# Attention's projection, value and output products as rolling pairs of row halves beside the scores

## The chip, the cores and the metric

The kernel runs on one core of a Trainium2 chip. The metric is the device time of one execution in microseconds (us), lower is better. Engines are named as in the profile: PE is TensorE's matmul, PEld its weight load, DVE is VectorE, ACT ScalarE, POOL GpSimd and SP SyncE, which issues DMAs.

## What is computed

Four layers in turn on x of 2048 rows and 512 columns, each added to its own input after a layer norm: a Fourier layer, an attention, the same Fourier layer, the same attention (`x = x + A(norm(x)); x = x + B(norm(x))`, twice). The Fourier layer is a product with two 512x512 matrices and then two 2048x2048 ones. The attention has 32 heads of 16 columns and four segments of 512 rows:

```python
q, k, v = x @ wq, x @ wk, x @ wv          # split into 32 heads, 4 segments
for s in range(4):
    p = softmax(qs @ ks.T * scale + mask)  # causal within the segment
    a_dot = p @ vs
    a_mem = (phi(qs) @ M) / (phi(qs) @ z + 1e-6)
    o = g * a_mem + (1 - g) * a_dot        # g = sigmoid(beta), per head
    M, z = M + phi(ks).T @ vs, z + sum(phi(ks))
return o @ wo
```

`phi(t)` is t + 1 above zero and exp(t) below.

## The kernel before

The program is laid out by hand on a clock of slots. `place(order, generator, times)` enters a generator at one or more times; at the end all entries run by time, and by `order` within a time, and each runs its generator up to the next `yield`. The matmuls and transposes are kept in the order in which they are so issued. The other engines' instructions are put in order by the compiler's scheduler, in which maxima and some copies have a raised priority. All PSUM tiles come from one pool of eight banks (`bank`).

The Fourier layers (`place_spectral`) are not touched. `place_attention` lays out one attention, from slot t0: 32 units of ten slots (SU = 10), a unit being four heads of one segment, so a segment (SS) is 80 slots. b is a segment's first slot. For each unit at slot t:

- `stack` (t-22) loads the heads' queries and keys with their low parts from DRAM, 48 rows for two heads at partition 0 and two at 64.
- `natural_max` computes scores with queries along partitions ("nat"), in five groups of two banks, and DVE takes each row's maximum with the mask (line 835). Two heads' matmuls run in the lower and upper half of the array's rows (`SIDES`).
- `max_rows` (t-5) turns the maxima into rows 48 and 49 of the query stack: a transpose `mT`, a copy `mt`, two DMAs.
- `softmax_values` computes the scores again, keys along partitions ("sT", 50 rows), in five groups at t, t+2, ..., t+8. ACT applies relu to the diagonal blocks and the exponential (lines 903, 904); POOL masks. At t+12 the 16 value products (`pv`, 32 output columns each, recorded as two matmuls apiece) follow, and a copy `ot`.
- `output` (t+14) transposes `ot` ("on") and divides.

For each segment there are `prep` (loads, normalises, transposes the rows into `xT`), `values` (four tiles `pvv`), `proj` (for four groups of heads g a tile each of q and k, `pqk`, followed by two copies, the feature map `phi` and DMAs to DRAM scratch), `mem_read` and `mem_update` (products with and into the state M, "pm", transposes "pkT", copy `pkn`, products "pM"), `transpose_out` ("oT") and `outproj` ("po", four tiles, plus the row added from `xr`). Numbers are held as a high and a low part, so each 128-row block takes three matmuls (`matmul3`), and a tile of 128x512 takes twelve. `matmul3` of projections, values and outputs stands three or six at a time in the slots between the scores, which are in every even slot.

The last segment of the second attention has its own tail (`outproj_split`, `transpose_last`), which is not changed.

Of the kernel before, what the change touches and what calls it, by code (L numbers as in the profile page):

```python
# [18 lines left out]
P = 128  # L19
# [39 lines left out]
def spectral_infini_kernel(  # L59
# [20 lines left out]
    def in_order(engine, name):  # L80
        op = getattr(engine, name)

        def call(*args, **kwargs):
            return tc.keep_in_program_order(op(*args, **kwargs))  # L84

        return call

    T = SimpleNamespace(matmul=in_order(T, "matmul"), transpose=in_order(T, "transpose"))
# [17 lines left out]
    def matmul3(ps, lhsT, rhs, first, last, **kw):  # L106
        T.matmul(ps, lhsT(0), rhs(0), start=first, stop=False, **kw)
        T.matmul(ps, lhsT(0), rhs(1), start=False, stop=False, **kw)
        T.matmul(ps, lhsT(1), rhs(0), start=False, stop=last, **kw)

# [570 lines left out]
    def place_attention(x_in, x_out, t0, w_at, out_at):  # L681
# [3 lines left out]
        def prep(s, n):  # L685
            xt = [load_rows(x_in[s * LT + i]) for i in n]
            yield
            mine = slice(s * LT + n[0], s * LT + n[-1] + 1)
            mv, rr = row_mv[:, mine], row_r[:, mine]
            if s == NSEG - 1:  # L690
                ve, r = row_stats(xt, mv)
            yield
            if s == NSEG - 1:
                row_scale(rr, ve, r)
                yield
            for j, i in enumerate(n):
                with behind_max():
                    xn = normal(xt[j], mv[:, j], rr[:, j : j + 1])
                yield
                if i == 0:  # L700
                    xT[s] = sb.tile([P, 2, DT, 512], F32R, name="xT", bufs=1)
                pt = bank("xnT", (P, DT, P))
                for d in range(DT):
                    T.transpose(pt[:, d], xn[:, d * P : (d + 1) * P], ident)
                sl = slice(i * P, (i + 1) * P)
                split(xT[s][:, 0, :, sl], xT[s][:, 1, :, sl], pt)
                if j + 1 < len(n):
                    yield
            yield

        def values(s):
            vt[s] = {}
            for i in (0, 1, 3, 2):
                ps = bank("pvv")
                for d in range(DT):
                    matmul3(
                        ps,
                        lambda h: xT[s][:, h, d, i * P : (i + 1) * P],
                        lambda h: ws["v", d][:, h, :],
                        d == 0,  # L720
                        d == DT - 1,
                    )
                    if d + 1 < DT:
                        yield
                j = v_count[0] % len(v_tiles)
                v, v_flat[s, i] = v_tiles[j], v_all[:, j]
                v_count[0] += 1
                A.activation(v[:, :, :DH], ps.rearrange("p (h d) -> p h d", d=DH), AF.Copy)
                vt[s][i] = v
                yield  # L730

        def proj(s, g, n):
            ps = bank("pqk")
            for d in range(DT):
                matmul3(
                    ps,
                    lambda h: ws[n, d][:, h, g * P : (g + 1) * P],
                    lambda h: xT[s][:, h, d, :],
                    d == 0,
                    d == DT - 1,  # L740
                )
                if d + 1 < DT:
                    yield

            def phi_tile():
# [65 lines left out]
        def natural_max(s, g, u):  # L811
# [3 lines left out]
            def scores(*cols):  # L815
                banks = [bank("nat") for _ in SIDES]
                views, off = [], 0
# [13 lines left out]
                for src, dst in views[::2] + views[1::2]:  # L831
                    n = src.shape[1]
                    junk = sb.tile([P, 512], BF16, name="junk", bufs=1)
                    with tc.high_priority(offset=URGENT):
# [3 lines left out]
                        )  # L838

# [19 lines left out]
        def max_rows(s, g, u):  # L859
            qs, parts = stacks[s, g, u, "q"], maxima.pop((s, g, u))  # L860
            pt = bank("mT")
            T.transpose(
                pt[:MCOLS, :P], parts.bitcast(F32), ident
            )
            n = MROWS * HU * LT
            mt = sb.tile([P, P], F32R, name="mt", bufs=2)
            with tc.high_priority(offset=URGENT):
                A.activation(mt[:n], pt[:n, :P], AF.Copy)
# [8 lines left out]
        def softmax_values(s, g, u):  # L877
# [4 lines left out]
            def scores(dst, *cols):  # L882
                banks = [bank("sT") for _ in SIDES]
                off, diag = 0, []
                for p, kt in cols:
                    n = 512 - kt * P
                    for a, at in enumerate(SIDES):
# [9 lines left out]
                for a, ps in enumerate(banks):  # L897
# [4 lines left out]
                    else:  # L902
                        A.activation(blocks, blocks, AF.Relu)  # L903
# [58 lines left out]
            def last():  # L962
# [5 lines left out]
                ot = sb.tile([P, 512], F32, name="ot", tag="ut", bufs=8)  # L968
                A.activation(ot, pb, AF.Copy)
                outs[s, g, u] = ot  # L970

            ev(12, last)
            for t in range(13):
                for f in events.get(t, ()):
                    f()
                yield

        def output(s, g, u):
            ot = outs.pop((s, g, u))
# [14 lines left out]
            for j in range(0, LT, 2):  # L994
# [5 lines left out]
                if s > 0:  # L1000
                    if j == 0:
                        tmps = sb.tile([P, LT, HU, DH], F32, name="otmp", tag="ut", bufs=8)
# [169 lines left out]
        for k in range(4 * DT):  # L1172
            n, d = "qkvo"[k // DT], k % DT
            src = rows((wq, wk, wv, wo)[k // DT], d)
            place(3, load_split(ws, (n, d), src, f"w{n}", "w", 16), [w_at(k) - 3, w_at(k)])
        for n in range(NSEG * USEG):
            t = t0 + SU * n
            place(0, softmax_values(*unit(n)), run_from(t, 13))
            place(1.9, output(*unit(n)), [t + 14])
            place(1.9, max_rows(*unit(n)), [t - (6 if x_out is out_tiles and n == NSEG * USEG - 1 else 5)])  # L1180
            place(1, natural_max(*unit(n)), run_from(t - 18, 5, 2), [t - 9])
            place(0.5, stack(*unit(n)), [t - 22])
        for s in range(NSEG):
            b = t0 + SS * s
            for j in range(2):
                t = b - (43, 51, 60, 60)[s] + 5 * j
                first = (12, 10, 6, 3) if s == NSEG - 1 else (10, 7, 5) if s == 1 else (8, 5, 3)
                place(2, prep(s, (2 * j, 2 * j + 1)), [*(t - d for d in first), t, t, t + 2])
            place(2, values(s), *([light(b - 20), light(b)] if s else [run_from(b - 18, 8), light(b - 10)]))
            place(2, alloc_out(s), [b - 13])  # L1190
            o = b + SS
            if s < NSEG - 1:
                free = light(o + 20) + light(o + 40) if s < NSEG - 2 else run_from(o + 20, DT * LT, 3)
            else:
                free = [out_at(k) for k in range(4 * LT)]
            if s == NSEG - 1 and x_out is out_tiles:
# [8 lines left out]
            for g in range(NG):  # L1205
# [5 lines left out]
                    (0, 2): among(b, b + 13, 8),  # L1211
                    (0, 3): among(b + 13, b + 29, 8),
                    (1, 0): among(b - 40, b - 29, 8),
                    (1, 1): among(b - 29, b - 17, 8),
                }.get((s, g), light(t - 50))
                place(2, proj(s, g, "q"), at[:4], post(at[3]))
                place(2, proj(s, g, "k"), at[4:], post(at[7]), late)
# [114 lines left out]
```

## Time and profile before

| what | value |
|---|---|
| median of three runs | 1785.14 us (1780.21 to 1789.34) |
| the profiled execution | 1787.75 us, its span 1786.0 us, mean granted clock 0.993 |
| value products `pv_bank` on PE | 2048 matmuls, 152.2 us busy |
| score groups on PE | `nat` 1024 matmuls, `sT` 1024 |
| maxima on DVE (line 835) | 1024 of mean 486 ns, 497.2 us |
| exponentials on ACT (line 904) | 640 of mean 612 ns, 351.3 us |

The profile is of one execution. Its span runs from the first to the last instruction. A matmul's end is modelled, and matmuls overlap, so the distance from one start to the next tells more than the length of one. In rows such as `nat<-stkk,stkq 48*128 48x512 x2` the words are the output, its inputs, the weights' rows and columns, the moving operand, and the number of instructions merged into the row. The first attention's scores run from about 429 to 903 us, the second's from 1304 to 1770.

### The profile page before, as it was taken

The numbers are of one execution on the slowest core, as the hardware profiler recorded it, in microseconds if no ns is written. First come the engines' busy times: TensorE is split into PE (matmuls) and PEld (weight loads), VectorE is DVE, ScalarE is ACT, GpSimd is POOL, SyncE is SP. The second block draws the span as 40 slices with busy tenths as digits, with TensorE's granted clock in tenths as the row PEclk, the third lists the DMA queues.
The fourth block names the chain that finished last, engine by engine and source line by source line (L and its number), as shares of the span: only waits on it lengthen the run. The fifth ranks groups of instructions, "written<-read, shape, count | busy, mean of one in ns | idle before, by whom it ended". The sixth has DMA issues, their size and how long they took to land. (4 is left out here: it accounts for less than half of the span.)

```text
span 1786.0 us, 32579 instructions
## 1 busy us (share of the span) xinstructions
PE 1745.4 (98%) x10192; PEld 1266.5 (71%) x10192; DVE 1383.1 (77%) x4114; ACT 1071.3 (60%) x2388; POOL 357.7 (20%) x673
## 2 busy tenths in 40 slices
PE   8999999999999999999999999999999999999998
PEld 6888777887656666666578888888875666666655
DVE  8888978864777888877977997667658778787775
ACT  3344443432688777777764665444328787877775
POOL 1000000002232334344410000000123333333332
PEclk9999999999999999999999999999999999999999
DMA  8787775355455454555666877645546555555351
GB/s 284 244 263 254 232 249 167 106 177 159 143 153 139 142 147 111 157 129 130 170 207 215 264 236 232 195 147 149 176 130 183 134 131 151 132 132 155 91 131 44
DMA packets 145499, 303.10 MB, mean 170 GB/s; under 512 B 18096, under 2 KB 22192, under 8 KB 145328
## 3 DMA queue, kind: packets, MB, share of 16 engines
q1 hardware_dynamic: 138416, 288.44, 54.7%
q10 hardware_dynamic: 6912, 12.59, 1.8%
q8 instruction: 82, 1.34, 0.3%
q14 instruction: 89, 0.73, 0.1%
HBM read 211.83 MB, written 88.08 MB: 168 GB/s over the span
## 5 line engine op out<-in xcount | busy, mean ns | idle before, releaser
L835 DVE CUSTOM_DVE_ANT_0 junk<-nat,mask 128x512 bf16<-128x512 f32 (+3 forms) x1024 | 497.2, 486 | 178.9 <-PE nat L84 133.4
L904 ACT ACTIVATE pT<-sT 128x512 f32<-128x512 f32 x640 | 351.3, 612 | 0.7
L84 PE MATMUL m<-chi,xa 128*128 128x512 f32 x1056 | 308.6, 392 | 2.5 <-DVE c L524 2.1
L907 POOL TENSOR_SCALAR_AFFINE_SELECT pT<-pT 128x256 f32<-128x256 f32 (+1 forms) x448 | 193.3, 445 | 566.5 <-ACT pT L904 434.0
L84 PE MATMUL m<-clo,xa 128*128 128x512 f32 x720 | 230.8, 392 | 5.5 <-DVE clo L100 5.5
L84 PEld LDWEIGHTS m<-chi,xa 128*128 128x128 f32 x1056 | 198.1, 189 | 46.6 <-DVE c L524 2.9
L903 ACT ACTIVATE sT<-sT 128x256 f32<-128x256 f32 x625 | 179.7, 331 | 64.4 <-PE sT L84 63.5
L84 PE MATMUL y<-wdt,us 128*128 128x512 f32 x768 | 182.5, 391 | 0.2 <-DVE wdt L100 0.2
L84 PE MATMUL nat<-stkk,stkq 48*128 48x512 f32 (+3 forms) x1024 | 159.2, 345 | 8.4 <-DMA stkk<-scrk 5.6
L84 PE MATMUL sT<-stkq,stkk 50*128 50x256 f32 (+3 forms) x1024 | 164.8, 373 | 1.0 <-DMA stkq<-mt 0.8
L84 PEld LDWEIGHTS y<-wdt,us 128*128 128x128 f32 x768 | 143.4, 188 | 30.7 <-DVE wdt L100 0.9
L84 PEld LDWEIGHTS sT<-stkq,stkk 50*128 50x128 f32 x1024 | 84.4, 186 | 113.4 <-issue 53.0
L84 PEld LDWEIGHTS m<-clo,xa 128*128 128x128 f32 x720 | 135.2, 188 | 37.8 <-DVE clo L100 10.0
L84 PE MATMUL pv_bank<-pT,v_all 128*32 128x512 f32 (+3 forms) x2048 | 152.2, 437 | 1.7 <-DVE mx L835 1.7
L98 ACT ACTIVATE chi<-cring 128x512 fp32r<-128x512 f32 (+1 forms) x138 | 99.6, 727 | 86.0 <-PE m L84 35.8
L84 PEld LDWEIGHTS pv_bank<-pT,v_all 128*32 128x32 f32 x2048 | 59.2, 110 | 84.1 <-issue 82.8
L84 PE MATMUL pqk<-xT,wq 128*128 128x512 f32 x384 | 116.9, 425 | 0.0
L84 PEld LDWEIGHTS nat<-stkk,stkq 48*128 48x128 f32 x1024 | 96.5, 189 | 27.2 <-ACT pT L904 7.7
L84 PE MATMUL po<-wo,oh 128*128 128x512 f32 x384 | 114.5, 419 | 0.7 <-ACT oh L98 0.5
L147 POOL TENSOR_TENSOR r<-ve,half_neg 128x2 f32<-128x2 f32 (+2 forms) x24 | 19.9, 830 | 472.9 <-DVE ve L145 469.5
L84 PE MATMUL pvv<-wv,xT 128*128 128x512 f32 x384 | 114.1, 417 | 0.0
L84 PE MATMUL pqk<-xT,wk 128*128 128x512 f32 x384 | 108.5, 410 | 2.0 <-DVE mx L835 2.0
(187 smaller groups left out, 2830.4 us busy)
## 6 DMA issues: line engine op xcount, KB each, us to landing
cring<-in_ct SPq DMA_DIRECT2D x97, 256.0 KB
scrk<-parts SPq DMA_DIRECT2D x96, 256.0 KB
stkq<-scrq SPq DMA_DIRECT2D x128, 192.0 KB
stkk<-scrk SPq DMA_DIRECT2D x128, 192.0 KB
cring<-sum SPq DMA_DIRECT2D x95, 256.0 KB
xt<-mid SPq DMA_DIRECT2D x64, 256.0 KB
scrq<-parts SPq DMA_DIRECT2D x32, 512.0 KB
cring<-in_ct SPq DMA_DIRECT2D x27, 512.0 KB
```

Of the source, the lines that this page charges most:

```text
L84: return tc.keep_in_program_order(op(*args, **kwargs))
L98: pin(A.activation(hi, src, AF.Copy, scale=scale))
L147: G.tensor_tensor(out=r, in0=ve, in1=half_neg[:, :n], op=ALU.pow)
L835: last_max[0] = V.tensor_tensor_reduce(junk[:, :n], src, mask[:, 512 - n :], 1.0, 3e38, ALU.add, ALU.min, dst,)
L903: A.activation(blocks, blocks, AF.Relu)
L904: A.activation(dst[a], ps, AF.Exp, scale=-SCALE)
L907: G.affine_select(blocks, blocks, pattern=[[0, n] for n in blocks.shape[1:-1]] + [[1, P]], compare_op=ALU.is_ge, fill=0.0, base=0, channel ...
```

## The change

It touches `place_attention` and some helpers. Projections, values and output products of the segments become *chains*: tiles in a fixed order, one every five slots, and each of a tile's twelve matmuls is split into the lower and the upper 64 rows of its operands (`half_product`). In each step (`chain_step`) the lower half of one tile and, 18 steps later (`LAG`), the upper half of the same tile are issued, so that a lower half of one tile stands beside the upper half of an earlier one, in another PSUM bank. The first upper matmul of a tile waits for the first reader (a maximum on DVE, or a relu on ACT) of a group of scores that was issued after the tile's last lower matmul (`evicted`, `add_manual_dep`).

```diff
+    def half_product(tile, side, n):
+        d, (i, j) = n // len(PASSES), PASSES[n % len(PASSES)]
+        at = slice(side * P // 2, (side + 1) * P // 2)
+        ins = T.matmul(
+            tile.ps,
+            tile.lhsT(d, i)[at],
+            tile.rhs(d, j)[at],
+            start=(side, n) == (0, 0),
+            stop=(side, n) == (1, DT * len(PASSES) - 1),
+            skip_group_check=True,
+        ).ins
+        if (side, n) == (1, 0):
+            behind = next(ins for at, ins in evicted if at > tile.at)
+            tc.add_manual_dep(ins, behind.name, SYNC, reason="both halves of the rows")
+        tile.at = issued[0]
...
+        STEPS = DT * len(PASSES)
+        LAG = STEPS * 3 // 2
+
+        def chain_step(k):
+            if k // STEPS in chain:
+                low = chain[k // STEPS]
+                if k % STEPS == 0:
+                    low.ps = bank(low.name)
+                    if hasattr(low, "begin"):
+                        low.begin()
+                half_product(low, 0, k % STEPS)
+            k -= LAG
+            if k // STEPS in chain:
+                half_product(chain[k // STEPS], 1, k % STEPS)
+            yield
...
+        def chain_time(k):
+            return t0 + 5 * (k // STEPS) + 2.2 + 4.6 * (k % STEPS) / (STEPS - 1)
```

A tile of the output products loads its row `xr` at its first step (`begin`), and `chain_tail` runs what follows a tile (copies, features, DMAs, or the row's end). A segment's sixteen tiles are in this order, with none in the places of the previous segment's outputs in the first segment, and none after the first six in the last. The first attention's and the second's q and k of group 2 of segment 0 stand in the two places ahead of the first segment. The remaining work of segment 0 and the outputs of the last segment stay whole products.

```diff
+            at = 2 * USEG * s
+            order = [chain_proj(s, 3, n) for n in "qk"]
+            order += [chain_out(s - 1, i) if s else None for i in range(LT)]
...
+            if s < NSEG - 1:
+                order += [chain_proj(s + 1, g, n) for g in range(2) for n in "qk"]
+                order += [chain_values(s + 1, i) for i in range(2)]
+                order += [chain_proj(s + 1, 2, n) for n in "qk"]
+                order += [chain_values(s + 1, i) for i in (3, 2)]
+            chain.update({at + h: tile for h, tile in enumerate(order) if tile})
```

What uses the whole array is put together at one time in each unit, slot 1.9: output transposes (`transpose_out`), the update's transposes, row transposes (`prep`), `output`, memory reads, the update's products, and last the value products, which leave `softmax_values`. `natural_max` moves by one slot to the odd slots, so that it no longer shares a slot with the other scores. The transposes of the maxima become two of 64 rows each, with a bank and a copy each:

```diff
+        def apart(s, k):
+            return t0 + SS * s + SU * k + 1.9
+
         for n in range(NSEG * USEG):
             t = t0 + SU * n
-            place(0, softmax_values(*unit(n)), run_from(t, 13))
-            place(1.9, output(*unit(n)), [t + 14])
-            place(1.9, max_rows(*unit(n)), [t - (6 if x_out is out_tiles and n == NSEG * USEG - 1 else 5)])
-            place(1, natural_max(*unit(n)), run_from(t - 18, 5, 2), [t - 9])
-            place(0.5, stack(*unit(n)), [t - 22])
+            final = n >= NSEG * USEG - 2
+            place(0, softmax_values(*unit(n)), run_from(t, 9))
+            place(0.9, value_products(*unit(n)), [t + (12 if final else 11.9)])
+            turned = t + 14 if n >= NSEG * USEG - 3 else t + 14.5 if n % USEG == USEG - 1 else t + 21.9
+            place(0.5, output(*unit(n)), [turned])
+            turn = t - (6 if x_out is out_tiles and n == NSEG * USEG - 1 else 5)
+            place(1.9, max_rows(*unit(n)), [turn])
+            place(1, natural_max(*unit(n)), run_from(t - 17, 5, 2), [t - 8])
+            place(0.6, stack(*unit(n)), [t - 22])
...
-            with tc.high_priority(offset=URGENT):
-                A.activation(mt[:n], pt[:n, :P], AF.Copy)
+            for a in SIDES:
+                at = slice(a, a + P // 2)
+                pt = bank("mT", (P, P // 2))
+                T.transpose(pt[:MCOLS], parts[at].bitcast(F32), ident[at, at])
+                with tc.high_priority(offset=URGENT):
+                    A.activation(mt[:n, at], pt[:n], AF.Copy)
...
                 if s > 0:
-                    place(2, mem_read(s, g), [t - 12, t - 8])
+                    place(0.6, mem_read(s, g), [apart(s, (0, 3, 5, 6)[g])] * 2)
                 if s < NSEG - 1:
-                    place(2, mem_update(s, g), [t + 5, t + 8] if g else [t + 16, t + 19])
+                    update = mem_update(s, g)
+                    place(0.3, update, [apart(s, (1, 4, 5, 7)[g])])
+                    place(0.7, update, [apart(s, (1, 4, 5, 7)[g])])
...
+        for k in range(STEPS * min(chain), STEPS * (max(chain) + 1) + LAG):
+            if k // STEPS in chain or (k - LAG) // STEPS in chain:
+                place(2, chain_step(k), [chain_time(k)])
+        for j in chain:
+            end = chain_time(STEPS * (j + 1) - 1 + LAG) + 0.05
+            place(2.1, chain_tail(j), [end, end + 1, end + 1.5, end + 2] if chain[j].name == "pqk" else [end])
```

The preparation of a segment's rows moves to the third and fourth unit of the segment before (from about slot b-51 or b-60). `ot` becomes a pair of buffers whose second half takes over from `otmp`.

More of the change, by code (lines that the diff above doesn't have):

```diff
@@ L732, in proj, with chain_tail @@
+        def chain_tail(j):
+            yield from chain[j].end(chain[j].ps)
         def proj(s, g, n):
@@ L816, in scores @@
                 banks = [bank("nat") for _ in SIDES]
+                start = issued[0] + 1
                 views, off = [], 0
@@ L886, in scores @@
                     n = 512 - kt * P
+                    last = issued[0] + 1
                     for a, at in enumerate(SIDES):
@@ L967, in last @@
                 pv(pb, 2, [p2[0][:, :, p] for p in range(HP)], 0)
[L968 to L969 removed]
+                ot = pair("ot", "ut", 8, F32)
+                A.activation(ot[:, 0], pb, AF.Copy)
                 outs[s, g, u] = ot
[L972 to L973 removed]
+            pending[s, g, u] = last
+            for t in range(9):
                 for f in events.get(t, ()):
```

114 lines of the change are left out of this document (81 added, 33 removed).

## The prediction

> **What bounds the kernel now.** I read the page first, then busy time by stage, then TensorE's instructions in order of time through one unit.
>
> ```profile
> span 1786.0 us, 32579 instructions
> PE 1745.4 (98%) x10192; PEld 1266.5 (71%) x10192; DVE 1383.1 (77%) x4114; ACT 1071.3 (60%) x2388; POOL 357.7 (20%) x673
> ```
>
> Busy time by stage follows; the columns are stage, length, and busy us (instructions) of PE, PEld, DVE, ACT and POOL, then clock and DMA. The stages are the four segments of the first attention and the four of the second, eight units each.
>
> ```profile
> 457.00:568.00 111.00, 107.61 (x759) 67.72 (x762) 85.23 (x347) 91.81 (x230) 36.84 (x66) 0.95 0.52 140
> 568.00:680.00 112.00, 111.94 (x834) 73.85 (x823) 91.26 (x366) 85.85 (x215) 39.66 (x77) 1.00 0.50 135
> 680.00:791.00 111.00, 109.89 (x817) 71.80 (x815) 91.94 (x371) 81.33 (x205) 39.48 (x76) 1.00 0.55 141
> 791.00:902.00 111.00, 105.89 (x742) 66.89 (x744) 95.51 (x357) 87.43 (x218) 46.27 (x85) 1.00 0.59 159
> 1332.00:1442.00 110.00, 106.43 (x757) 66.97 (x759) 85.35 (x346) 91.53 (x229) 36.84 (x66) 0.97 0.52 141
> 1442.00:1552.00 110.00, 109.94 (x823) 72.47 (x816) 86.94 (x348) 83.79 (x210) 36.46 (x73) 1.00 0.51 134
> 1552.00:1662.00 110.00, 108.93 (x790) 71.96 (x788) 89.55 (x359) 83.00 (x208) 40.03 (x77) 1.00 0.55 146
> 1662.00:1770.00 108.00, 103.16 (x771) 63.94 (x770) 80.89 (x336) 79.57 (x198) 38.98 (x84) 0.98 0.37 92
> ```
>
> Both attentions (445 + 438 us) are TensorE's: in the second and third segments it has hardly a gap. The spectral stages are untouched. A unit takes 111 / 8 = 13.9 us. But a busy PE is not PE at its peak, so what does it do in a unit? TensorE in order of time, start and length first:
>
> ```profile
> 618.31 0.94 PE L84 MATMUL pqk<-xT,wq 128*128 128x512 f32 x3
> 619.18 0.50 PE L84 MATMUL sT<-stkq,stkk 50*128 50x512 f32 x2
> 619.52 0.40 PE L84 MATMUL nat<-stkk,stkq 48*128 48x512 f32 x2
> 619.85 0.66 PE L84 MATMUL oT<-ident,onat 128*128 128x128 f32 x4
> 620.27 1.63 PE L84 MATMUL pqk<-xT,wk 128*128 128x512 f32 x6
> 621.83 0.50 PE L84 MATMUL sT<-stkq,stkk 50*128 50x512 f32 x2
> 622.17 0.45 PE L84 MATMUL nat<-stkk,stkq 48*128 48x128 f32 x4
> 622.55 1.65 PE L84 MATMUL pqk<-xT,wk 128*128 128x512 f32 x6
> 624.13 0.50 PE L84 MATMUL sT<-stkq,stkk 50*128 50x256 f32 x4
> 624.47 0.40 PE L84 MATMUL nat<-stkk,stkq 48*128 48x256 f32 x4
> 624.80 1.68 PE L84 MATMUL po<-wo,oh 128*128 128x512 f32 x6
> 626.32 0.60 PE L84 MATMUL oT<-ident,onat 128*128 128x128 f32 x4
> 626.84 2.36 PE L84 MATMUL pv_bank<-pT,v_all 128*32 128x512 f32 x32
> 629.13 0.51 PE L84 MATMUL sT<-stkq,stkk 50*128 50x384 f32 x4
> 629.48 0.50 PE L84 MATMUL nat<-stkk,stkq 48*128 48x512 f32 x2
> 629.91 0.97 PE L84 MATMUL po<-wo,oh 128*128 128x512 f32 x3
> 630.81 0.50 PE L84 MATMUL sT<-stkq,stkk 50*128 50x384 f32 x4
> 631.15 0.50 PE L84 MATMUL nat<-stkk,stkq 48*128 48x128 f32 x4
> 631.58 0.66 PE L84 MATMUL on<-ident,ot 128*128 128x128 f32 x4
> 632.08 0.27 PE L84 MATMUL mT<-ident,mparts 128*72 128x128 f32 x1
> ```
>
> From start to start, three whole-array products take 0.87 us (618.31 to 619.18) and six take 1.56 (620.27 to 621.83): 0.23 each, and 0.18 per stretch is lost at its ends. The five stretches last 0.87 + 1.56 + 1.58 + 1.52 + 0.90 = 6.43 us, of which 24 x 0.23 = 5.52 is streaming: **0.9 lost**. The five visits to the scores (48 or 50 rows, two heads side by side in the halves of the array) last 0.67 + 0.72 + 0.67 + 0.78 + 0.77 = 3.61. Each visit streams 1,024 columns per half, 0.46 at the same rate, 2.30 in all: **1.3 lost**. A 128-column matmul takes longer than its columns: with a transpose at about 0.11 against 0.06, the four such pairs keep 0.2 of that. So about 2.0 of 13.8 us, or 0.4 per round trip between whole array and halves, go into changing over, five times a unit.
>
> **The change, part by part.**
>
> *Chains in halves (removes).* Each 128-row product of the projections, values and output becomes two 64-row ones: the lower half of one tile beside the upper half of the tile before, 18 steps behind. Scores, chains and the two half transposes of the maxima then all use the array in halves; whole-array work and value products stand once a unit, at 1.9 of its ten time slots. Of five round trips one is left: 5 x 0.4 - 0.4 = 1.6 us a unit, 64 units: **-102**. This needs a pair of 64-row halves of 512 columns to take 0.23 like one whole product. No such pair stands in a long row here; the nearest is the visit at 624.13, where four pairs of 256 columns and a round trip's loss take 0.67 (4 x 0.115 = 0.46). Bounds: 0.22 (all hidden) and 0.46 (one after the other). I take 0.23.
>
> Here a rule of the Trainium skill speaks against the change. "TensorE: Matmul & The Clock Gate", Part 3, The mechanism, says that a weight load overlaps running matmuls only when the row group differs. By it each step would show its load, since both halves are always running; the same section also allows the background weight buffer. The visit at 624.13 speaks against it: four pairs with four loads fit in 0.67 us, while 4 x (0.115 + 0.11) = 0.90 would be needed if a load showed for the 0.11 of a transpose.
>
> *Lone halves (adds).* Where a row of tiles starts or ends, one half runs alone for 18 steps. Per attention there are two rows (tiles -2 to 1, then 6 to 53), so four in all, each 18 steps longer: 4 x 18 x 0.23 = **+17**.
>
> *Maxima (adds).* Two half transposes and two copies in place of one each. The first row below is the copy's group (count, busy us and mean ns); the second, from the order of time, is for the part after this one.
>
> ```profile
> L868 ACT ACTIVATE mt<-mT 32x128 fp32r<-32x128 f32 x64 | 16.5, 258 | 7.2 <-PE mT L84 7.2
> 633.58 0.60 ACT L1051 ACTIVATE pkn<-pkT 128x512 f32<-128x512 f32 x1 [0.48 <-PE pkT L84]
> ```
>
> On TensorE at most one 128-column transpose more, 0.1 x 64 = **+6**. The second copy, 0.26 x 64 = 17 us of ScalarE, lies in that engine's idle time (111 less its busy time, 19 to 30 us a segment); without that cover it costs those 17.
>
> *Memory update (moves, adds a wait).* Its transposes and its products, three slots apart before, now stand in one slot. Between them lie at times only the four `on` transposes, 0.49 us (631.58 to 632.08). The copy `pkn` between them takes 0.60, after the transposes' 0.27 drain and behind up to two exponentials. TensorE waits at least 0, at most some 1.2; I take 0.5, 24 times (4 groups, 3 segments, 2 attentions): **+12**. Queued behind it are the value products and all scores.
>
> *The wait of the second half.* The first upper step of a tile waits for an eviction of scores that were issued after the last lower step. Six steps lie between, 2.5 slots or some 3.2 us. Queued behind it are all of TensorE's scores, hence VectorE and ScalarE.
>
> ```profile
> 629.96 0.69 DVE L835 CUSTOM_DVE_ANT_0 junk<-nat,mask 128x512 bf16<-128x512 f32 x1 [0.22 <-PE nat L84]
> ```
>
> From the pair's start at 629.48 to the end of this first maximum is 1.2 us with VectorE idle; the next group is issued up to 1.3 later, so it starts to cost when VectorE is 0.7 behind. Bounds 0 and 0.5 us for each of 104 tiles, 0 to +52. I take **+4**.
>
> *Buffers and queues.* A chain tile holds its bank for 30 steps, 12.5 slots, so two a unit hold 2.5 of 8 banks all the time; a score group takes two. This may cost TensorE waits in the segments that now have none; the first and last of the first attention, with ScalarE at 83% and VectorE at 86%, have 3 and 5 us of gaps. I take **+6**, bounds 0 and 77 (below). The output's row loads (`xr`) are issued at a tile's start, about 12 slots before their use, through SP, and hold one of five buffers meanwhile. If none is free, the stack loads queue behind them on SP. Those now have five slots instead of four before use, so I take 0; at 1 us for each of 24 loads it would be 24. The other moves (slots of preparation, memory reads, output transposes) keep their instructions: 0, within these bounds.
>
> *Sum.* -102 + 17 + 6 + 12 + 4 + 6 = **-57**. The profiled execution took 1787.75 (span 1786.0); the median of the runs is 1785.14, 2.6 lower. 1785 - 57 = **1728 us**. A unit would then be about 13.0 us; VectorE's fullest segment, 95.51 / 8 = 11.9, lies under it. So the engine late next is VectorE, at about 92%, with ScalarE close.
>
> **Rivals.**
>
> *Waits eat the gain.* The second half's wait at 0.5 us for 104 tiles gives back 52 of 57: 1780. For it: VectorE would have little slack, and a whole-array block of about 4 us lets no scores be made, after which VectorE and ScalarE are fed in bursts. Against: 3.2 us of distance.
>
> *Slower: banks run out.* With 2.5 banks in chains and one in the block's work, two score groups fill the rest, and TensorE waits in order until an older group is read. Then the lag from a pair's start to its first maximum, 0.48 us (629.48 to 629.96), is no longer covered. In half of the five rounds it costs 1.2 us a unit, 77 in all: 1805. From 57 / (64 x 5) = 0.18 us a round this decides. The Trainium skill ("TensorEngine Tiling (Array Packing)", PSUM Bottleneck) likewise says that tiling speeds up the array but not the emptying of PSUM. For it: each nat group's maxima are VectorE's largest work. Against: the page shows VectorE idle a fifth of the time.
>
> *The change doesn't do what it says: the halves don't run side by side.* Loads not hidden (the rule above): 0.11 for 52 tiles x 12 steps x 2 = 1,248 steps, +137, 1865; or halves in turn, 1,248 x 0.23 = +287, 2015. Against: the visit at 624.13.
>
> **Chances.** Forecast with its spread (1685 to 1770) 0.65; waits eat the gain (1770 to 1795) 0.16; banks run out 0.14; halves not side by side 0.05. The forecast's lower end is no waits (-22) and 20 us of present TensorE gaps filled. Range: 1685 to 1795. About 0.5% (9 us) is what a measurement can tell from no change; of the second case some 0.06 lies below 1776. Faster 0.71, same 0.10, slower 0.19.
>
> **What would show it.** Right: in units of the second segment, chain steps at 0.23 us between scores with one whole-array block a unit, a unit of about 13.0 us, VectorE over 85% busy. Wrong: steps at 0.34 or 0.46; TensorE idle ahead of a chain matmul with VectorE or ScalarE as releaser (the second half's wait), ahead of scores (banks), or ahead of `pM` by over 0.5 us.

## The result and the profile after

The changed kernel takes 1838.14 us (median; 1835.12 to 1843.37), the kernel before 1784.86 in the same comparison: a ratio of 1.030 (95% interval 1.027 to 1.034). It is **slower by 53 us**, where 57 less were forecast; the time lies outside the range. The profiled execution took 1843.37 us against 1787.75, so the traces have to account for 55.6.

The page of the changed kernel, its span, its engines and the group of the `sT` scores (busy us, mean ns | idle time of the engine before them, and what ended most of it):

```profile
span 1841.7 us, 35419 instructions
PE 1751.0 (95%) x11504; PEld 1332.9 (72%) x11504; DVE 1389.4 (75%) x4114; ACT 1076.4 (58%) x2452; POOL 362.8 (20%) x673
...
L86 PE MATMUL sT<-stkq,stkk 50*128 50x256 f32 (+3 forms) x1024 | 196.0, 356 | 21.8 <-ACT pT L999 17.2
```

The same group on the page of the kernel before:

```profile
L84 PE MATMUL sT<-stkq,stkk 50*128 50x256 f32 (+3 forms) x1024 | 164.8, 373 | 1.0 <-DMA stkq<-mt 0.8
```

Before, TensorE stood idle 1.0 us ahead of these scores, and for a DMA. Now it is 21.8, mostly for ACT's exponential `pT`, which reads the bank that the next scores need. Busy time by stage of the changed kernel, the segments of the first attention and the last of the second (columns as before):

```profile
462.00:586.00 124.00, 115.08 (x981) 81.62 (x981) 89.98 (x360) 97.40 (x250) 39.38 (x71) 0.94 0.48 134
586.00:708.00 122.00, 113.87 (x1052) 83.07 (x1051) 95.51 (x380) 90.80 (x230) 41.37 (x79) 1.00 0.50 132
708.00:832.00 124.00, 114.21 (x1063) 83.99 (x1063) 98.94 (x400) 88.62 (x229) 44.12 (x85) 1.00 0.49 130
832.00:932.00 100.00, 92.51 (x682) 62.54 (x682) 83.57 (x304) 72.86 (x188) 38.90 (x71) 0.90 0.56 157
...
1720.00:1826.00 106.00, 98.47 (x805) 67.37 (x802) 78.40 (x323) 73.97 (x193) 36.91 (x81) 0.90 0.37 94
```

The middle segments, which had hardly a gap, now have 8 to 10 us of gaps each. A unit of the second segment takes 122 / 8 = 15.3 us instead of the forecast 13.0. VectorE is at 78%, not at the forecast 85% or more: no engine has become the bound, all of them wait more. In the last segments the granted clock is 0.90, where it was 1.00 and 0.98. TensorE through parts of one unit, in order of time:

```profile
662.46 0.25 PE L86 MATMUL mT<-ident,mparts 64*72 64x64 f32 x1
663.10 0.25 PE L86 MATMUL mT<-ident,mparts 64*72 64x64 f32 x1 [0.39 <-ACT pT L999]
...
664.42 0.39 PE L86 MATMUL pvv<-wv,xT 64*128 64x512 f32 x1
664.42 0.39 PE L86 MATMUL pqk<-xT,wk 64*128 64x512 f32 x1
664.65 0.38 PE L86 MATMUL pvv<-wv,xT 64*128 64x512 f32 x1
664.65 0.38 PE L86 MATMUL pqk<-xT,wk 64*128 64x512 f32 x1
664.88 0.40 PE L86 MATMUL nat<-stkk,stkq 48*128 48x512 f32 x2
665.12 0.40 PE L86 MATMUL pvv<-wv,xT 64*128 64x512 f32 x1
665.12 0.40 PE L86 MATMUL pqk<-xT,wk 64*128 64x512 f32 x1
...
665.60 0.40 PE L86 MATMUL sT<-stkq,stkk 50*128 50x512 f32 x1
666.61 0.50 PE L86 MATMUL sT<-stkq,stkk 50*128 50x512 f32 x1 [0.62 <-ACT pT L999]
666.61 0.72 PE L86 MATMUL pvv<-wv,xT 64*128 64x512 f32 x2
```

The chains do what was forecast: pairs of chain halves start at 664.42 and 664.65 and the pair of scores behind them at 664.88, each 0.23 after the last, the two halves side by side and their loads hidden. But between two halves of one transpose 0.64 us pass (662.46 to 663.10), and between two halves of one score group 1.01 (665.60 to 666.61). Both rows name the exponential `pT` as what they waited for, the reader of a bank of scores, and the chains behind them wait too. What TensorE waited for between 440 and 940 us (total us, times, longest), in the changed kernel:

```profile
PE sT L86 <- ACT pT L999: 8.5, 15, 0.6
PE mT L86 <- ACT pT L999: 8.3, 19, 1.3
PE pM L86 <- ACT pkn L1152: 6.0, 9, 1.8
PE nat L86 <- DVE mx L925: 1.4, 3, 0.6
```

and in the kernel before, the first rows of the same view:

```profile
PE xnT L84 <- DVE xn L168: 2.6, 2, 1.7
PE nat L84 <- DMA stkk<-scrk: 1.7, 4, 0.6
PE pv_bank L84 <- DVE mx L835: 1.7, 1, 1.7
```

**An account of both traces.** A view of waits shows only what it can name, so I also added up TensorE's matmul starts, from the last product of the Fourier layer to the last value products, both attentions together. A stretch is a run of one kind (whole array, value products, chains, scores, half transposes); its time to the next stretch's start, less its streaming (512 columns at 0.2325 us, one of two halves and a record of a value product at half of that, a whole-array matmul of 128 or 136 columns some 0.025 more than its columns), is its loss. Time that the clock gate took (length times one minus the granted clock) is taken off first. Stretches at full clock in which no start comes over 0.25 us later than the columns of the matmul ahead of it account for give the usual loss of their kind; what the others lose beyond that is put down as waits. Waits below 0.25 us remain in the losses, so the line between the two is a choice: with 0.10 in its place the losses inside the halves below come to about 42 instead of 69.

| us | streaming | losses on entering and leaving the whole array | losses between chains, scores and transposes inside the halves | waits | low clock | sum |
|---|---|---|---|---|---|---|
| before | 716.4 | 164.2 (702 changes) | 0 | 31.2 | 10.2 | 922.0 |
| after | 713.4 | 59.5 (260) | 69.2 (1530) | 102.4 | 32.5 | 977.0 |
| difference | -3.0 | **-104.7** | **+69.2** | **+71.2** | **+22.3** | +55.0 |

The sums differ by 55.0, as the executions do (55.6). So by this account the saving came, and three things ate it. About four fifths of the loss inside the halves lie between chains and scores, the rest around the half transposes. The experiments ask whether these are what they look like; their accounts are in one table at the end of the next section.

### The profile page after: what moved, and what is told of

Its sections match the earlier page's. It is cut to its first block, busy times and chain, and to the rows that moved or that the text cites. A ratio compares the mean times of both kernels' runs of the same rounds, so it can differ in the third digit from the quotient of the medians.

```text
span 1841.7 us, 35419 instructions
## 1 busy us (share of the span) xinstructions
PE 1751.0 (95%) x11504; PEld 1332.9 (72%) x11504; DVE 1389.4 (75%) x4114; ACT 1076.4 (58%) x2452; POOL 362.8 (20%) x673
## 5 line engine op out<-in xcount | busy, mean ns | idle before, releaser
L86 PE MATMUL sT<-stkq,stkk 50*128 50x256 f32 (+3 forms) x1024 | 196.0, 356 | 21.8 <-ACT pT L999 17.2
L86 PE MATMUL pqk<-xT,wq 64*128 64x512 f32 (+1 forms) x720 | 214.8, 406 | 0.0
L86 PE MATMUL pqk<-xT,wk 64*128 64x512 f32 (+1 forms) x720 | 208.0, 396 | 0.0
L86 PE MATMUL nat<-stkk,stkq 48*128 48x384 f32 (+3 forms) x1024 | 196.8, 344 | 7.9 <-DVE mx L925 2.6
L86 PE MATMUL pvv<-wv,xT 64*128 64x512 f32 (+1 forms) x672 | 192.7, 405 | 0.0
L86 PEld LDWEIGHTS sT<-stkq,stkk 50*128 50x128 f32 x1024 | 118.4, 189 | 99.7 <-ACT pT L999 33.8
L86 PEld LDWEIGHTS nat<-stkk,stkq 48*128 48x128 f32 x1024 | 137.2, 191 | 36.6 <-DVE mx L925 10.3
L86 PEld LDWEIGHTS m<-clo,xa 128*128 128x128 f32 x720 | 135.2, 188 | 37.5 <-DVE clo L103 8.9
L86 PE MATMUL po<-wo,oh 64*128 64x512 f32 (+1 forms) x672 | 155.4, 402 | 0.6 <-ACT oh L101 0.5
L1064 ACT ACTIVATE ot<-pv_bank 128x512 f32<-128x512 f32 x64 | 38.4, 601 | 191.1 <-PE pv_bank L86 185.5
L86 PEld LDWEIGHTS pqk<-xT,wk 64*128 64x128 f32 (+1 forms) x720 | 121.2, 187 | 7.9 <-issue 2.2
```

The source lines that it names most:

```text
L1064: A.activation(ot[:, 0], pb, AF.Copy)
```

## The experiments

Each time below is a median, with its ratio to the kernel before measured beside it and the 95% interval.

**Banks.** If the waits are for banks, taking one of the eight away must hurt the changed kernel much more than the kernel before. An otherwise unused tile holds it through each attention, in both kernels:

```diff
+    def hold():
+        t = bank("held")
+        T.transpose(t[:, :P], ident, ident)
+        yield
+        with tc.issue_after(last_max[0].ins):
+            V.tensor_copy(held, t[:, :1])
+        yield
...
+    place(5, hold(), [b1, b1 + LB - 20])
+    place(5, hold(), [b2, b2 + LB - 20])
```

> The kernel before, with one of the eight PSUM banks held by an unused tile through each attention. Banks theory (the changed kernel is slower because TensorE waits for banks): the kernel before has banks to spare, so under +10 us (1785 to 1795). Theory that the one whole-array block per unit starves VectorE and ScalarE, and banks don't matter: 0 to +5.

> The changed kernel with one of the eight banks held in the same way. Banks theory: it already runs short, so one bank less costs at least 40 us (1880 or more). Block theory: at most +10 (1848).

Before with a bank less: 1803.03 us, 1.011 [1.010, 1.013], 20 us more than the kernel before beside it (1783.26). After with a bank less: 1945.11, 1.091 [1.088, 1.093], 107 more than the change. What TensorE waited for in the changed kernel with a bank less, whole span:

```profile
PE mT L86 <- ACT parts L854: 19.1, 26, 0.7
PE mT L86 <- ACT pT L999: 18.5, 42, 0.9
PE nat L86 <- DVE mx L925: 13.2, 30, 0.6
```

The half transposes `mT`, each with a bank of its own, wait most, for whichever reader happens to free a bank. The kernel before lost more than the 10 us expected, so it had no whole bank to spare, but it could do without one far better; the change has used up what was spare.

The other side: let the readers free banks earlier. These two leave out the relu (exponential's scale divided by 256), which takes some 620 operations off ACT:

```diff
-                        done = A.activation(blocks, blocks, AF.Relu)
...
-                    A.activation(dst[a], ps, AF.Exp, scale=-SCALE)
+                    done = A.activation(dst[a], ps, AF.Exp, scale=-SCALE / 256)
```

> The kernel before with the same left out. Both theories: TensorE sets its time, so at most 10 us faster (1775 or more). If it gains as much as the changed kernel, ScalarE was a bound of both.

> The changed kernel without the relu before the exponentials, and with the softmax scale divided by 256 to keep them finite: 640 short ScalarE instructions fewer, score banks come free sooner, TensorE's work is the same. Banks theory, with ScalarE releasing them: 50 us or more faster (1790 or less). Theory that TensorE itself is slower in halves (skewed pairs, loads that show): at most 15 faster.

Before: 1783.42, 0.999 [0.997, 1.000], no change. After: 1802.38, 1.010 [1.007, 1.013], 36 us faster than the change, which lies between the 50 that the one theory expected and the 15 of the other. In the account 37 us of waits go and 7 of low clock. ACT is busy 58% of the span, yet its work is now on TensorE's path, through the banks.

**Can the banks be had back by rearranging?** Six single edits, one each, to the changed kernel: a shorter lag between a tile's halves (15 steps instead of 18, so that it holds its bank for less time), a longer one (24), a whole `mT` with one bank at the end of the whole-array block, the high part of k and q copied from their first copy and no longer from PSUM, relu and exponential at raised priority, every second relu on VectorE.

```diff
-        LAG = STEPS * 3 // 2
+        LAG = STEPS * 5 // 4        # after_lag15; STEPS * 2 in after_lag24
...
+            pt = bank("mT")         # after_mt_block, at t - 8.1, natural_max one slot earlier
+            T.transpose(pt[:MCOLS, :P], parts.bitcast(F32), ident)
...
-            A.activation(parts[:, 0], ps, AF.Copy, scale=sign)
+            A.activation(parts[:, 0], raw, AF.Copy)   # after_parts_raw
...
+                        with tc.high_priority(offset=URGENT):   # after_exp_urgent, both
+                            done = A.activation(blocks, blocks, AF.Relu)
...
-                    if x_out is out_tiles and (s * NG + g) * NU + u >= NSEG * USEG - 3 and a:
+                    if a:                              # after_relu_dve
                         V.tensor_scalar_max(blocks, blocks, 0.0)
```

> The changed kernel with the upper halves 15 steps behind instead of 18: a chain tile holds its bank for 27 steps instead of 30 (2.25 banks instead of 2.5). Banks theory: 10 to 25 us faster than the changed kernel (1813 to 1828). Theory that the second half's wait for an eviction is the cost: slower by 10 or more, as only 3 steps instead of 6 lie between. Block theory: within 5.

> The changed kernel with the upper halves 24 steps behind: 36 steps a tile, 3.0 banks. Banks theory: 20 to 50 us slower (1858 to 1888), 6 of them the longer lone halves. Second half's wait: faster by 10 or more. Block theory: within 10.

> The changed kernel with the maxima's transpose whole again (one bank, one copy), as the last of the whole-array block, and natural_max back in its old slots. Banks theory: the second half transpose waits 0.58 us for a bank in each unit, so 25 to 50 us faster (1788 to 1813). If the waits only move to the next instruction that needs a bank: within 10 of the changed kernel.

> The changed kernel with the second copy of a projection taken from the first copy instead of from its bank, so that the bank comes free one copy (about 0.5 us) sooner. Banks theory: 5 to 30 us faster. Theory that ScalarE's time as such is the bound: within 5, since ScalarE does as many copies.

> The changed kernel with relu and exponential at the raised priority of the maxima, so that on ScalarE they go ahead of copies and features and the score banks come free sooner. Banks theory, if the order on ScalarE is the trouble: 10 to 30 us faster. If ScalarE's amount of work is: within 7.

> The changed kernel with every second relu on VectorE instead of ScalarE (320 of 640; VectorE is idle a quarter of the span). Banks theory with ScalarE as the one that releases late: 10 to 30 us faster. If VectorE's share is as tight (its maxima wait behind these): same or slower.

| edit | us | ratio to before |
|---|---|---|
| after_lag15 | 1857.3 | 1.041 [1.040, 1.043] |
| after_lag24 | 1862.84 | 1.044 [1.043, 1.046] |
| after_mt_block | 1867.8 | 1.047 [1.044, 1.050] |
| after_parts_raw | 1844.99 | 1.034 [1.031, 1.036] |
| after_exp_urgent | 1838.96 | 1.031 [1.029, 1.034] |
| after_relu_dve | 1846.96 | 1.036 [1.034, 1.038] |

None is faster than the change. After_parts_raw has 16 us more waits in the account, and 13 less of low clock and losses inside the halves; with the whole `mT` the waits go up by 6 and the low clock by 15. Four of the six missed what the banks theory expected of them: the shorter lag (10 to 25 us faster expected, 19 slower measured), the whole `mT` (25 to 50 faster, 30 slower), after_parts_raw (5 to 30 faster, 7 slower) and after_relu_dve (10 to 30 faster, 9 slower). So holding a bank for less time, or reading it sooner in one place, did not help; these edits also move other work, and why the shorter lag is slower stays open. That the second half's wait then costs, as another theory had it, is not borne out by the longer lag, which it expected to be faster and which is 25 slower. In after_parts_raw, for one, `sT` waits for `pT` rise from 17.2 to 23.9 us.

**The placement without the halves.** The change also moves work: all else of the whole array into one block, `pM` right behind its transposes, two tiles of each attention ahead of its first segment. So: the same placement, tiles as whole 128-row products in five stretches a unit (`after_whole`); the change with `pM` one block later (`after_pm_next`); and both kinds with `pM` later and the two early tiles put back (`whole_pm_lead`, `halves_pm_lead`).

```diff
-                half_product(low, 0, k % STEPS)
-            k -= LAG
-            if k // STEPS in chain:
-                half_product(chain[k // STEPS], 1, k % STEPS)
+                n = k % STEPS                          # whole: after_whole, whole_pm_lead
+                d, (i, j) = n // len(PASSES), PASSES[n % len(PASSES)]
+                T.matmul(low.ps, low.lhsT(d, i), low.rhs(d, j), start=n == 0, stop=n == STEPS - 1)
...
-            return t0 + 5 * (k // STEPS) + 2.2 + 4.6 * (k % STEPS) / (STEPS - 1)
+            n, tile = k % STEPS, k // STEPS
+            return t0 + 5 * (tile + 1) + ((3.5, 5.5)[n // 6] if tile % 2 else (2.5, 4.5, 6.85)[n // 4])
...
-                    place(0.7, update, [apart(s, (1, 4, 5, 7)[g])])
+                    place(0.7, update, [apart(s, (1, 4, 5, 7)[g] + 1)])      # pm
...
-                chain.update({k - 4: chain_proj(0, 2, n) for k, n in ((2, "q"), (3, "k"))})
+                    (0, 2): among(b, b + 13, 8),                             # lead
```

> The changed kernel with the chains as whole 128-row products again, in five stretches a unit of 4 to 6 beside the one whole-array block; all else as changed. A tile holds its bank for 12 steps, and five round trips a unit are back. Banks theory: the bank waits go and the changeovers return, so close to the kernel before, 1775 to 1805. Block theory (one whole-array block a unit is what starves the other engines): 1830 or more.

> The changed kernel with the memory update's products one block after its transposes, so that they no longer wait for the copy between (the trace shows 6.0 us of such waits in the first attention's stretch). If each wait counts once: 8 to 14 us faster than 1838. If TensorE only waits elsewhere instead: within 5.

> No halves: whole products in the change's placement, pM one block later, and the first projections of an attention put back where the kernel before has them. If the waits for pkn (about 26 us in all) and the longer lead (about 15) explain what the placement costs: about 1800 us. If it is the order inside a block: stays above 1820.

> The changed kernel with pM one block later and the first projections of an attention put back where the kernel before has them. If the two tiles and the lone halves in the lead cost about 10 us per attention: 1806 to 1816 us. If what the lead does is only regained elsewhere: within 5 us of 1826.

| edit | us | ratio to before |
|---|---|---|
| after_whole | 1845.34 | 1.035 [1.032, 1.038] |
| after_pm_next | 1825.89 | 1.024 [1.022, 1.027] |
| whole_pm_lead | 1807.24 | 1.011 [1.008, 1.014] |
| halves_pm_lead | 1827.23 | 1.022 [1.019, 1.025] |

`pM` behind its transposes costs the change 12 us. By after_whole alone the halves would cost nothing (1845 against 1838), as the theory of the block expected. But without halves TensorE waits longer for the copy `pkn`, 29.2 us against 12.1 in the changed kernel. What it waited for most in after_whole, whole span:

```profile
PE pM L86 <- ACT pkn L1151: 29.2, 23, 2.6
```

The two early tiles: halves_pm_lead is within 2 us of after_pm_next, so my reading that they and their lone halves cost 10 us per attention fell. From the last product of the Fourier layer to the first `sT` each attention takes 11.2 us instead of 15.6, but its first segment takes 5 us longer. And with `pM` and the lead out of the way, **whole products are 20 us faster than halves** (1807 against 1827): the halves save 84 at the array's changes, and lose 53 inside and 52 in waits. The placement alone, whole_pm_lead, is still 22 us above before. In the account 20.6 of that is the clock. So, by runs alone and in this order, 11 of the 53 us are `pM` and the early tiles, 20 the halves and 22 the placement.

**Is the saving there once the scores' banks come free early?** The two kernels without the relu, and with every maximum read from the last 128 columns of its scores alone (this leaves out most of the maxima's work), so that VectorE too frees banks early:

```diff
-                            junk[:, :n], src, mask[:, 512 - n :], 1.0, 3e38,
+                            junk[:, :P], src[:, n - P :], mask[:, 512 - P :], 1.0, 3e38,
```

> The kernel before without the relu (scale over 256) and with each row maximum read from the last 128 columns of its scores only, so that ScalarE and VectorE drain the score banks early. Before hardly waits for banks, so both theories expect 1765 to 1784 us.

> The changed kernel with the same two omissions. Theory A, that the halves' saving in changeovers is whole and waits for banks hide it: at least 40 us below the kernel before with these omissions, some 1730. Theory B, that the saving itself is small (about 50 us) and lead, lone halves and waits for pkn eat it: within 15 us of that kernel.

Before: 1771.85 us, 0.991 [0.987, 0.994]. After: 1782.24, 0.997 [0.995, 0.999], so 10 us above it. Theory A fell, and theory B's condition is met, though not by B's reason. At the array's changes 100 us are saved; 62 are lost inside the halves, 35 more in waits and 12 in clock. The waits for the readers of scores have gone from the top of the list:

```profile
PE pM L86 <- ACT pkn L1148: 9.5, 20, 1.1
PE sT L86 <- DMA stkq<-mt: 8.2, 13, 1.8
PE sT L86 <- ACT parts L854: 7.3, 27, 0.4
```

First are now `pM` for its copy and the scores for their row of maxima, on its way through transpose, copy and DMA. The third row is still a wait for a bank: `parts` is the second reader of a projection's tile. So this pair of runs doesn't show the halves with no wait for banks at all.

**Is the loss inside the halves a price of each alternation?** Chain steps issued four at a time, and six at a time with `pM` a block later:

```diff
-            return t0 + 5 * (k // STEPS) + 2.2 + 4.6 * (k % STEPS) / (STEPS - 1)
+            return t0 + 5 * (k // STEPS) + 2.2 + 4.6 * (k % STEPS // 4 * 4) / (STEPS - 4)
```

> The changed kernel with the chain steps issued four at a time, so that scores and chain steps alternate about a third less often. If each alternation inside the halves costs its 0.08 us in the trace (0.06 after scores, 0.02 after chains): some 200 fewer of them, about 15 us off, 1823 us, and the sum of these losses in the trace falls from about 60 us to 45. If the loss belongs to the score groups themselves, or waits take its place: within 6 us of 1838.

> Six chain steps at a time, so that they alternate with scores about half as often, and pM one block later (1826 without the longer runs). By the price of an alternation about 1802 us. If longer runs of chains starve VectorE and ScalarE, or make waits for banks behind them: 1820 or more.

Slower: 1879.31, 1.054 [1.050, 1.057], and 1982.02, 1.111 [1.108, 1.114]; for the first neither theory expected this. The alternations fall from 1530 to 1053 and 605, but the loss inside stays at 75 and 64 us, so it isn't one fixed price for each. Whether the scores keep it whatever stands beside them is not shown. By a like count, whose totals lie within 6 us of the table's, it is between scores and chains alone about 58 us in 1389 passages in the changed kernel, 60 in 912 in burst4 and 31 in 482 in burst6_pm. There it grows around the half transposes to some 38, an estimate from few stretches (12 of 123 are free of waits). Meanwhile the waits rise to 119 and 183. First rows of the waits of burst6_pm, whole span:

```profile
PE nat L86 <- ACT pT L999: 30.6, 59, 0.9
PE sT L86 <- DVE mx L925: 22.3, 32, 0.8
PE sT L86 <- ACT parts L854: 16.6, 26, 0.7
```

The accounts of all that the text compares:

| us | changes of the array | inside the halves | waits | low clock |
|---|---|---|---|---|
| before | 164.2 | 0 | 31.2 | 10.2 |
| after | 59.5 | 69.2 | 102.4 | 32.5 |
| before_bank_less | 169.9 | 0 | 37.5 | 11.9 |
| after_bank_less | 59.0 | 81.9 | 176.4 | 52.9 |
| after_norelu | 59.1 | 74.1 | 65.6 | 25.6 |
| after_parts_raw | 58.1 | 61.3 | 117.9 | 27.3 |
| after_mt_block | 70.4 | 60.8 | 108.1 | 47.8 |
| after_pm_next | 59.4 | 69.6 | 91.3 | 29.1 |
| after_whole | 145.0 | 12.8 | 77.6 | 29.1 |
| whole_pm_lead | 147.2 | 15.6 | 37.1 | 30.8 |
| halves_pm_lead | 63.0 | 68.6 | 89.4 | 30.8 |
| before_light | 157.9 | 0 | 21.6 | 15.3 |
| after_light | 58.1 | 62.4 | 56.8 | 27.3 |
| burst4 | 59.0 | 75.3 | 118.7 | 46.1 |
| burst6_pm | 54.3 | 63.5 | 182.7 | 100.7 |

No version that does the whole work is faster than the kernel before.

## Why the prediction was wrong

Its sum was -57. Term by term, account less forecast: -57 - 2.7 (the changes) + 46.2 (inside) + 49.2 (waits) + 22.3 (clock) - 3.0 (streaming) = +55.0.

*Chains in halves*: half right. The pair step takes 0.23 and the round trips that go save 105, where 102 were forecast. That these agree so well is luck: four of five round trips a unit, 256 in all, were to go at 0.4 us each; by the account about 223 go (1.5 a unit are left, not one), at 0.47 each. What failed is the step before it: all that a visit to the scores loses was read as changing over, bar 0.2 a unit, so that passing between scores and chains inside the halves was put at nothing. Of the 69 us now lost inside the halves, the forecast had 17 for *Lone halves* (worked out from the same 144 steps, not measured apart) and at most 6 for *Maxima*; the other 46 are 0.7 us a unit. They aren't one fixed price per alternation; how they divide between the scores' own starts, the passages and waits too short for the account stays open. Taken by runs, halves_pm_lead against whole_pm_lead, the halves cost 20 us, where the sum without *Memory update* had them save 69.

*Buffers and queues*: the mechanism named, the size wrong. It was put at +6 within 0 to 77, *Memory update* at +12, *the wait of the second half* at +4, 22 together; the waits grew by 71. `pM` accounts for 12 by its own experiment, the size forecast. The second half's wait is about nothing: no chain matmul stands among the first rows of the waits. Of the rest, nearly 60, the views name some 38 as waits for readers of banks, by `sT`, `mT`, `nat` and the block's `pm` (42 in the changed kernel, 4 before), nearly all of them for `pT`; and 37 go with the relu. So banks come to about half of the upper bound, six times what was taken. What the remaining 20 wait for isn't named. I had counted 2.5 banks for the chains, but set the cost by what gaps the full segments had, when the kernel could still do without a bank for 20 us. I had also not counted that the two `mT` halves take two banks where one was taken; but with one bank for both (after_mt_block) the kernel was no faster.

The rival *banks run out* (1805, chance 0.14) had the right mechanism but the wrong reader: it priced the lag to VectorE's maxima, and TensorE waits for ScalarE's exponentials (37 us, against 5 for the maxima). Its 77 is near the 71 by which all waits grew, which is in part luck, as only about half of them are shown to be for banks; that it missed by 33 is the loss inside the halves and the clock. The Trainium skill's "TensorEngine Tiling (Array Packing)", PSUM Bottleneck, which was named with it, agrees: the readers of PSUM did not get faster (an exponential took 612 ns before and 604 after, a maximum 486 and 488). *Waits eat the gain* named the wrong wait. *Halves not side by side* fell, and with it the Trainium skill's rule that a load hides only behind another row group ("TensorE: Matmul & The Clock Gate", Part 3, The mechanism): each half's next load was hidden at 0.23 us a step.

*Not in the forecast at all*: the clock. The last segments have chains in their first six places only, and with the rest of the work in one block a unit TensorE has little to stream there while the maxima and exponentials are made. Of the 22 us, 19 lie in these two segments. The last segment of the first attention in the changed kernel, in 10 us windows:

```profile
872.00:882.00 10.00, 9.10 (x63) 6.22 (x63) 9.48 (x36) 7.68 (x21) 5.83 (x11) 0.88 0.68 161
882.00:892.00 10.00, 8.89 (x59) 5.58 (x51) 9.15 (x41) 7.82 (x23) 5.37 (x10) 0.67 0.59 156
892.00:902.00 10.00, 9.28 (x64) 5.14 (x62) 6.96 (x34) 4.61 (x15) 2.58 (x6) 0.77 0.78 239
902.00:912.00 10.00, 8.72 (x59) 5.43 (x61) 9.82 (x42) 6.00 (x15) 3.35 (x7) 0.66 0.32 106
```

VectorE is the busiest engine in most of these windows, TensorE gets gaps, and the granted clock drops to about two thirds. Gaps alone don't do it: in the kernel before, a window of the same segment shows a busier VectorE and more gaps at full clock.

```profile
872.00:882.00 10.00, 8.32 (x67) 4.67 (x66) 9.82 (x34) 8.36 (x22) 3.81 (x7) 1.00 0.67 216
```

What sets the two apart is how much is streamed (last section): columns fill 65% of the 3.41 us from 877.4 in the kernel before, and 38% of those from 883.0 in the changed one, behind which the clock is halved. In the changed kernel the 32 value products, which took 2.36 us at 626.84 before, then take longer:

```profile
657.27 2.36 PE L86 MATMUL pv_bank<-pT,v_all 128*32 128x512 f32 x32
...
894.11 3.59 PE L86 MATMUL pv_bank<-pT,v_all 128*32 128x512 f32 x32
```

Before, whole products stood between the scores up to the end, and the clock in this segment was 1.00. That whole_pm_lead, which has none of the halves, keeps 20.6 us of low clock and is 22 slower than before, points to the placement for this term; a version with the last segment's work spread out again was not tried.

## What to carry to other kernels

A change that saves switching on one engine should be costed by the buffers it holds meanwhile: count the banks of every tile in flight at the fullest slot, and if the count reaches all of them, put a price on each release that was hidden before. Ask of a measured loss to which neighbour it belongs before it is booked as saved; here time was still lost between scores and chains, with nothing left to switch. And work that is taken out of the thin stages of a program leaves them with little to stream, which here cost twice, as the clock was then halved.

## What the hardware showed that I had not expected

- The clock falls in stretches that look busy. The profile shows 0.50 over a whole 5 us window in which PE counts as busy 4.87:

```profile
885.00:890.00 5.00, 4.08 (x16) 2.08 (x16) 4.57 (x22) 4.91 (x16) 1.96 (x6) 0.64 0.24 65
890.00:895.00 5.00, 4.87 (x28) 3.76 (x31) 4.32 (x26) 1.89 (x5) 1.91 (x4) 0.50 0.99 222
```

  Each half-clock stretch within these traces lasts 3.41 us or a multiple of it. I cut both attentions of the kernel before and of the changed one into windows of that length, set on the edges of these stretches, and took the 527 windows at full clock. All 9 in which the matmuls' columns, at 0.2325 us per 512, fill under 35% of the time are followed by half clock, 4 of the 10 between 35 and 45%, and none of the 508 above. Busy time doesn't tell them apart: windows busy 80 to 90% are among those followed by half clock, and ahead of seven of the nine stretches in the changed kernel's attentions the longest gap in the window before was 0.73 us or less. The Trainium skill ("TensorE: Matmul & The Clock Gate", Part 1) describes a clock gate that follows how busy the array has been, with half rate as its lower state; half rate is what the trace shows. Waits thus cost more than their length: from after to burst6_pm the waits grew by 80 us and the low clock by 68.
- One bank of eight was worth 20 us to the kernel before and 107 to the changed one.
